# Smaller last pieces of the output projection, alternating stores, and V of three units in two transfers

## The chip, the cores and the metric

The kernel runs on one core of a Trainium2 chip. The metric is the device time of that core in microseconds (us). Each timed execution also has a span, from the first to the last instruction of the program; the time is about 1.8 us longer than the span (187.37 against 185.60 in the profiled run of the kernel before).

Engine names in the profile: PE is TensorE matmul, PEld its weight loads, DVE is VectorE, ACT is ScalarE, POOL is GpSimd, SP is SyncE. A "q" behind an engine's name (SPq, ACTq) marks its sequencer: issues of transfers, waits and branches.

## The reference, cut to what matters

```python
B, Sq, D = 8, 32, 1024;  Hq, Hkv, Sk, Dh = 32, 4, 8192, 128
q = (x @ wq).reshape(B, Sq, Hq, Dh).transpose(0, 2, 1, 3)
k = repeat(k_cache[:, :, Sk - W:, :], rep=8, axis=1)      # W = 2048: a window at the end of the cache
v = repeat(v_cache[:, :, Sk - W:, :], rep=8, axis=1)
p = softmax(einsum("bhqd,bhkd->bhqk", q, k) * Dh ** -0.5)
o = einsum("bhqk,bhkd->bhqd", p, v)
return o.transpose(0, 2, 1, 3).reshape(B, Sq, Hq * Dh) @ wo     # 256 rows x 1024 columns
```

All is bf16. The kernel cuts attention into 32 units, one for each pair of a batch and a KV head.

## The kernel before

For every unit, V (512 KB) is loaded in one transfer and copied by VectorE into an operand with a column of ones beside it:

```python
def load_v(self, ui, eng):
    b, g = self.units[ui]
    self.v_sb[ui] = self.vp.tile([self.P, self.KT, self.Dh], BF16, name="v_sb", tag="v")
    eng.dma_start(out=self.v_sb[ui][:, :, :],
                  in_=self.v_cache[b, g, self.Sk - self.W:, :].rearrange("(p j) d -> p j d", j=self.KT))
```

The output projection adds up over four head groups in an fp32 tile. In the last group a piece of columns is multiplied (8 matmuls into a PSUM tile `ps` from a pool of two), added to what was there, and stored:

```python
            if i == 0:
                st["ps"] = self.open_ps = self.ps_m.tile([P, 512], FP32, name="op_ps", tag="m")   # ps_m: 2 buffers
            # ... two of the piece's eight matmuls ...
            if i == 3 and mm is not True:
                # ...
                    o_t = self.osb.tile([P, 512], BF16, name="o_t")                               # osb: 5 buffers
                    nc.vector.tensor_tensor(out=o_t[:, 0:w], in0=ps[:, 0:w], in1=acc, op=ALU.add)
                    eng = nc.sync if n0 == 0 else nc.scalar
                    eng.dma_start(out=self.out[t * P:(t + 1) * P, n0:n0 + w], in_=o_t[:, 0:w])
```

The last block (the second 128 rows) comes last of all, in three pieces, and a branch stands in it. The kernel computes the softmax without subtracting the maximum; a check over all units decides whether an exact fallback has to run. Every engine passes this branch behind the matmuls of the first piece; with this data the fallback is skipped.

```python
    self.last = self.o_pieces(self.Hkv - 1, 1, (512, 256, 256))
    for p in self.last[:3]:
        p()
    self.last[3](mm=True)            # matmuls of the first piece, ahead of the branch
    # ... branch over the fallback ...
    self.last[3](mm=False)           # its add and store, behind the branch
    for p in self.last[4:]:
        p()
```

## Time and profile before

The first three runs had a median of 187.43 us (187.19 to 187.6). Numbers of the profiled run:

| what | value |
|---|---|
| span | 185.60 us |
| first score matmul starts | 13.65 us |
| start of the first to end of the last score matmul ("the middle") | 160.75 us |
| end of the last score matmul to first matmul behind the branch | 6.08 us |
| first matmul behind the branch to the end ("the tail") | 5.12 us |

The tail of the kernel before in order of time. Columns: start in us, length, engine, line, operation, output and inputs, shapes, count; in brackets the idle time before it and what ended that:

```profile
180.48 1.91 PE L290 MATMUL op_ps<-wo_sb,OT 128*128 128x256 bf16 x16
181.09 0.35 SPq L302 DMA_DIRECT2D out_dram<-o_t  x1
181.55 0.42 DVE L300 TENSOR_TENSOR o_t<-op_ps,oacc 128x256 bf16<-128x256 f32 x1 [0.49 <-PE op_ps L290]
182.01 1.21 ACTq L302 DMA_DIRECT2D out_dram<-o_t  x2
182.42 0.42 DVE L300 TENSOR_TENSOR o_t<-op_ps,oacc 128x256 bf16<-128x256 f32 x1 [0.45 <-PE op_ps L290]
```

The last store is the second of the two ScalarE issues, from 182.88 to 183.22. Its landing, from the list of transfers issued in that window (KB each, then us from issue to landing):

```profile
out_dram<-o_t ACTq DMA_DIRECT2D x1, 64.0 KB, 1.6
```

The trace's records have it to two digits: issued 182.88, landed 184.46. The record of a transfer covers its issue alone (0.34 us). The Trainium skill says so of this kind of transfer ("Perfetto Trace Analysis", section on the HWDGE DMA instruction: the movement of the data is not in the profiled window), and this trace agrees: 1.58 us from issue to landing, more than four times the record. The trace's packet records split these 1.58 us: the first packet starts 0.85 us after the issue began (0.51 us after the record has ended), the packets take 0.34 us, and the landing is seen 0.40 us after the last of them.

```profile
L646 SPq EVENT_SEMAPHORE  x5: 28/28/28, 184.5 to 184.7; - x5
L646 SPq DRAIN  x1: 13/13/13, 184.8 to 184.8; - x1
```

These are five waits: the one that the landing released, and four more whose semaphores were long there.

### The profile page before, as it was taken

To read this page: it belongs to the slowest core of one execution; us is meant where nothing else is said; L and a number is where in the kernel's file an instruction comes from. 1 tells how busy PE (TensorE), PEld (TensorE's weight loads), DVE (VectorE), ACT (ScalarE), POOL (GpSimd) and SP (SyncE) were. 2 spreads that over 40 slices of the span, in tenths; PEclk is the share of its full clock that TensorE was granted. 3 is DMA by queue.
4 is the path that set the end of the run, shared out by engine and by line. 5 is a ranking of instruction groups with operands and counts; after the bars stand their busy time and mean duration, and the time that the engine had idled before them with its cause. 6 is when DMAs were issued, how large, how long until landed. Compare 5 with 4: busy or idle time off the path is not lost. (4 is left out here: it accounts for less than half of the span.)

```text
span 185.6 us, 5054 instructions
## 1 busy us (share of the span) xinstructions
PE 178.8 (96%) x2048; PEld 153.1 (82%) x2064; DVE 115.1 (62%) x267; ACT 131.7 (71%) x133; POOL 94.7 (51%) x150
## 2 busy tenths in 40 slices
PE   7699999999999999999999999999999999999993
PEld 2589999999999999987878999987777888888842
DVE  0128699994586685586467558647746855445372
ACT  2207899787789777777777677787777888888700
POOL 2000007949939959929954980796299189500000
PEclk9999999999999999999999999999999999999999
DMA  6999999999999999999999999999999999930012
GB/s 151 321 397 415 414 415 389 195 270 353 296 274 304 310 320 398 368 240 254 376 323 250 367 349 276 202 409 357 269 371 329 192 326 174 276 96 0 4 62 62
DMA packets 52507, 51.75 MB, mean 279 GB/s; under 512 B 39424, under 2 KB 40064, under 8 KB 52480
## 3 DMA queue, kind: packets, MB, share of 16 engines
q1 hardware_dynamic: 51904, 50.87, 95.6%
q10 hardware_dynamic: 576, 0.52, 0.8%
q8 instruction: 17, 0.28, 0.6%
q14 instruction: 10, 0.08, 0.2%
HBM read 41.42 MB, written 0.52 MB: 226 GB/s over the span
## 5 line engine op out<-in xcount | busy, mean ns | idle before, releaser
L466 ACT ACTIVATE pT<-s_ps 128x1024 bf16<-128x1024 f32 x128 | 128.9, 1025 | 33.3 <-PE s_ps L464 32.3
L256 POOL TENSOR_SCALAR kTv<-kb 32x512 bf16<-32x512 bf16 x140 | 93.7, 670 | 65.4 <-DMA k_raw<-in_k_cache_dram 27.0
L475 PEld LDWEIGHTS <-pT 128*128 128x128 bf16 x1024 | 68.5, 98 | 3.1
L464 PEld LDWEIGHTS <-kT 128*128 128x128 bf16 x368 | 34.8, 98 | 10.3
L290 PE MATMUL op_ps<-wo_sb,OT 128*128 128x512 bf16 (+1 forms) x120 | 32.8, 365 | 0.8
L270 PE MATMUL q_ps<-xT,wq_sb 128*128 128x256 bf16 x192 | 28.2, 273 | 0.0
L475 PE MATMUL o_ps<-va_112,pT 128*128 128x129 bf16 x352 | 27.1, 220 | 0.0
L475 PE MATMUL o_ps<-va_113,pT 128*128 128x129 bf16 x352 | 27.0, 220 | 0.1
L475 PE MATMUL o_ps<-va_114,pT 128*128 128x129 bf16 x320 | 24.7, 220 | 0.0
L246 DVE STREAM_TRANSPOSE kb<-k_raw 128x512 bf16<-128x512 bf16 x36 | 23.8, 684 | 0.0
L412 DVE RECIPROCAL RL_all<-o_ps 128x2 f32<-128x2 f32 x32 | 5.2, 164 | 27.5 <-PE o_ps L475 27.5
L417 DVE TENSOR_SCALAR o_sb<-o_ps,RL_all 128x128 bf16<-128x128 f32 x64 | 19.5, 346 | 1.1
L464 PEld LDWEIGHTS <-kTv 128*128 128x128 bf16 x144 | 13.9, 98 | 5.1
L270 PEld LDWEIGHTS <-wq_sb 128*128 128x128 bf16 x192 | 17.0, 98 | 1.2
L464 PE MATMUL s_ps<-QT_63,kT 128*128 128x256 bf16 x112 | 16.8, 273 | 0.0
L419 DVE STREAM_TRANSPOSE OT<-o_sb 128x256 bf16<-128x256 bf16 x32 | 14.2, 445 | 1.1
L464 PE MATMUL s_ps<-QT_66,kT 128*128 128x256 bf16 x96 | 14.4, 273 | 0.1
L290 PEld LDWEIGHTS <-OT 128*128 128x128 bf16 x136 | 11.1, 98 | 2.8 <-DVEq L77 0.6
L464 PE MATMUL s_ps<-QT_65,kT 128*128 128x256 bf16 x80 | 12.0, 273 | 0.1
L464 PE MATMUL s_ps<-QT_64,kT 128*128 128x256 bf16 x80 | 12.0, 272 | 0.1
L297 DVE TENSOR_TENSOR oacc<-op_ps,oacc 128x512 f32<-128x512 f32 x8 | 5.5, 682 | 7.4 <-PE op_ps L290 7.4
L406 DVE COPY va_113<-v_sb 128x2048 bf16<-128x2048 bf16 x11 | 9.5, 859 | 0.0
(46 smaller groups left out, 104.0 us busy)
## 6 DMA issues: line engine op xcount, KB each, us to landing
v_sb<-in_v_cache_dram SPq DMA_DIRECT2D x32, 512.0 KB, 7.0
wo_sb<-in_wo_dram SPq DMA_DIRECT2D x16, 512.0 KB, 6.3
wq_sb<-in_wq_dram SPq DMA_DIRECT2D x14, 512.0 KB, 7.1
k_raw<-in_k_cache_dram SPq DMA_DIRECT2D x13, 512.0 KB, 5.7
wq_sb<-in_wq_dram SPq DMA_DIRECT2D x4, 256.0 KB, 7.0
kT<-in_k_cache_dram SPq DMA_TRANSPOSE x36, 6.9
k_raw<-in_k_cache_dram SPq DMA_DIRECT2D x2, 256.0 KB, 8.2
x_sb<-in_x_dram ACTq DMA_DIRECT2D x1, 256.0 KB, 3.7
```

The costliest lines, as they stand in the source:

```text
L246: nc.vector.transpose(out=st["kb"][:, sl, :], in_=self.k_raw[ui][:, sl, :])
L256: nc.gpsimd.tensor_scalar(out=out, in0=in_, scalar1=1.0, scalar2=1.0, op0=ALU.mult, op1=ALU.mult)
L270: nc.tensor.matmul(st["ps"][:, 0:self.NQ], lhsT=self.wq_t[g, i][:, c % (DC // 2), hl * P:(hl + 1) * P], rhs=self.xT[:, c, :], start=(c == ...
L290: nc.tensor.matmul(ps[:, 0:w], lhsT=self.OT[:, gq, c, t * P:(t + 1) * P], rhs=self.wo_t[gq][:, c, n0:n0 + w], start=(k == 0), stop=(k == 7))
L297: nc.vector.tensor_tensor(out=acc, in0=ps[:, 0:w], in1=acc, op=ALU.add)
L406: self.nc.vector.tensor_copy(out=self.va[ui % 3][:, :, 0:self.Dh], in_=self.v_sb[ui][:, :, :])
L412: nc.vector.reciprocal(out=rl[:, ui * QT_N:(ui + 1) * QT_N], in_=o_ps[:, :, Dh])
L417: nc.vector.tensor_scalar(out=o_sb[:, qt, :, :], in0=o_ps[:, qt, 0:Dh].rearrange("p (i c) -> p c i", c=4), scalar1=rl[:, ui * QT_N + qt:ui ...
L419: nc.vector.transpose(out=self.OT[:, g * QT_N:(g + 1) * QT_N, :, b * self.Sq:(b + 1) * self.Sq], in_=o_sb[:, :, :, :])
L464: nc.tensor.matmul(s_ps[:, jj, :], lhsT=self.kT[ui][:, c * CJ + jj, :], rhs=q_u, start=True, stop=True)
L466: nc.scalar.activation(out=pT[:, :, :], in_=s_ps[:, :, :], func=ACT.Exp, bias=0.0, scale=self.scale)
L475: nc.tensor.matmul(o_ps[:, qt, 0:self.VW], lhsT=pT[:, jj, qt * P:(qt + 1) * P], rhs=va[:, j, 0:self.VW], start=(j == 0 and qt == 0), stop= ...
```

## The change

Its intent, as far as the code tells: let the last add and the last store be small, so that little stands between the last matmul and the end; spread the stores over two issuing engines; and cut V of the last three units in two. It also rewrites the projection in the fallback as a loop over 32 heads, with another layout for the attention output that it reads; this is a much shorter program that doesn't run here.

```diff
+V_HALVES = 29
     def load_v(self, ui, eng):
-        eng.dma_start(out=self.v_sb[ui][:, :, :],
-                      in_=self.v_cache[b, g, self.Sk - self.W:, :].rearrange("(p j) d -> p j d", j=self.KT))
+        n = self.KT // (2 if ui >= V_HALVES else 1)
+        for j in range(0, self.KT, n):
+            eng.dma_start(out=self.v_sb[ui][:, j:j + n, :],
+                          in_=self.v_cache[b, g, self.Sk - self.W:, :].rearrange("(p j) d -> p j d", j=self.KT)[:, j:j + n, :])
@@ o_pieces
-                    eng = nc.sync if n0 == 0 else nc.scalar
+                    eng = nc.sync if n0 in (0, 768) else nc.scalar
@@ tail_begin
-        self.last = self.o_pieces(self.Hkv - 1, 1, (512, 256, 256))
+        self.last = self.o_pieces(self.Hkv - 1, 1, (512, 256, 128, 128))
@@ out_proj (fallback; cut)
-        with tc.For_i(0, Hkv, 1) as g:
-            # ... 8 heads of a group: one load, one copy, 32 matmuls
+        with tc.For_i(0, Hq, 1) as h:
+            # ... one head: one load, one copy, 4 matmuls
```

More of the change, by code (lines that the diff above doesn't have):

```diff
@@ L580, in attention_exact @@
                 nc.tensor.matmul(o_ps[:, :], lhsT=v_sb[:, j, :], rhs=pT[:, j, :], start=(j == 0), stop=(j == KT - 1))
-            nc.vector.tensor_copy(out=OT_e[:, bass.ds(g * (B * UQ) + b * UQ, UQ)], in_=o_ps[:, :])
+            nc.vector.tensor_copy(out=OT_e[:, :].rearrange("p (g h b s) -> p g h b s", g=Hkv, h=rep, b=B)[:, bass.ds(g, 1), :, bass.ds(b, 1), :],
+                                  in_=o_ps[:, :].rearrange("p (g h b s) -> p g h b s", g=1, h=rep, b=1))
 def out_proj(tc, wo, OT_e, out_flat, fast, *, Hkv, Hq, Sq, NQ, D):
@@ L596, in out_proj @@
         pc = ctx.enter_context(tc.tile_pool(name="pc", bufs=1, space=PSUM))
-        wo_v = wo.rearrange("(g h p) n -> g p h n", p=P, h=rep)
+        wo_v = wo.rearrange("(h p) n -> h p n", p=P)
         acc = accp.tile([P, NT, D], FP32, name="acc")
         nc.vector.memset(acc[:, :, :], 0.0)
-        with tc.For_i(0, Hkv, 1) as g:
-            wo_sb = wop.tile([P, rep, D], BF16, name="wo_sb")
-            nc.sync.dma_start(out=wo_sb[:, :, :], in_=wo_v[bass.ds(g, 1), :, :, :].rearrange("o p h n -> p (o h) n"))
-            o_g = wop.tile([P, rep, B, Sq], BF16, name="o_g")
-            nc.vector.tensor_copy(out=o_g[:, :, :, :].rearrange("p h b s -> p b h s"),
-                                  in_=OT_e[:, bass.ds(g * (B * UQ), B * UQ)].rearrange("p (b h s) -> p b h s", b=B, h=rep))
-            o_v = o_g[:, :, :, :].rearrange("p h b s -> p h (b s)")
-            ps = pc.tile([P, NT, D], FP32, name="ps")
-            for h in range(rep):
-                for t in range(NT):
-                    for n in range(NC_):
-                        nc.tensor.matmul(ps[:, t, n * 512:(n + 1) * 512], lhsT=o_v[:, h, t * P:(t + 1) * P],
-                                         rhs=wo_sb[:, h, n * 512:(n + 1) * 512], start=(h == 0), stop=(h == rep - 1))
+        with tc.For_i(0, Hq, 1) as h:
+            wo_sb = wop.tile([P, D], BF16, name="wo_sb")
+            nc.sync.dma_start(out=wo_sb[:, :], in_=wo_v[bass.ds(h, 1), :, :].rearrange("o p n -> p (o n)"))
+            o_h = wop.tile([P, NQ], BF16, name="o_h")
+            nc.vector.tensor_copy(out=o_h[:, :], in_=OT_e[:, bass.ds(h * NQ, NQ)])
+            ps = pc.tile([P, NT, D], FP32, name="ps")
+            for t in range(NT):
+                for n in range(NC_):
+                    nc.tensor.matmul(ps[:, t, n * 512:(n + 1) * 512], lhsT=o_h[:, t * P:(t + 1) * P],
+                                     rhs=wo_sb[:, n * 512:(n + 1) * 512], start=True, stop=True)
             nc.vector.tensor_tensor(out=acc[:, :, :], in0=ps[:, :, :], in1=acc[:, :, :], op=ALU.add)
```

## The prediction

> What bounds the kernel. The page's busy shares put PE at 178.8 of 185.6 us (96%); in every stretch that I read between 100 and 176 us PE is busy 98 to 100% at a clock of 1.00, and in the view of waits for 100 to 186 us PE waits for nothing. Only the tail is not PE: the last matmul group ends at 182.40, the last add (128x256, 0.42 us) at 182.84, the last store (64 KB, from ScalarE) is issued at 182.9 and lands 1.6 us later, about 184.5; closing waits take the rest to 185.6. So the change can act only by starving PE or on these last 3 us.
>
> V in halves (units 29 to 31). Same bytes, three more issues on SyncE of 0.38 to 0.53 us each (timeline of the DMA issues), rows of 2 KB for 4 KB. The copy into the V operand still waits for both halves, so nothing starts earlier. Issued, landed, copied: V29 148.5, 156.1, 162.2; V30 151.5, 159.9, 164.6; V31 159.7, 163.5, 170.1. The last half of K, issued at 160.3 and landed 164.6, is first read at about 172.5. Slack is 4.7 to 8 us against at most 1.5 us of added issue time: 0 us on the critical path.
>
> Last block 512, 256, 128, 128. 16 matmuls of 128 columns replace 8 of 256. The 256-wide ones are spaced about 0.107 us (16 in 1.91 us, less a 0.17 us pipeline tail), the 129-wide ones of the attention about 0.057 us (8 in 0.62 us): 0.91 us in place of 0.86. But the PSUM pool has two buffers: the fourth piece takes the buffer of the 256 piece, whose add ends at 181.97, while PE would be ready at about 181.80: a new wait of about 0.2 us. Estimate: the fourth piece runs 182.03 to 182.65, its add takes about 0.29 us (0.69 for 512 columns, 0.42 for 256, extrapolated) and ends about 182.95 in place of 182.84. The last add also reuses an output tile (five buffers, now six tiles), whose store, issued at 176.9, has long landed: 0.
>
> Stores. One more of 32 KB on SyncE at about 182.3, the last 32 KB on ScalarE at about 183.0. Before, the ScalarE issues (0.34 us each) stand 0.9 us apart, so alternating removes no queueing. The Trainium skill ("DMA: Bandwidth & Descriptors", Anatomy of one DMA) says the fixed cost of a DMA is mostly completion; the trace agrees: 64 KB lands in 1.6 us, of which the data burst is about 0.6. Half the bytes saves an estimated 0.1 us; its Specifications table says that rows under 512 B are read, modified and written, and the new rows are 256 B, so even that may not come. No run here shows it yet.
>
> The rest of the diff is the fallback branch, not executed on this data; it shortens PE's program by about 56 instructions.
>
> Sum: PE and PSUM wait +0.1, store -0.1 to +0.1, V 0: about +0.05 us. Predicted 187.5 us, range 186.9 to 188.1; faster by over 2%: 1%, within 2%: 98%, slower by over 2%: 1%.
>
> What would show it: V copies within 0.3 us of their times and no new PE wait before 176; last PE group ending near 182.6 after a wait for the 256 add; last add of about 0.29 us ending at 182.8 to 183.0; last landing 1.4 to 1.7 us after issue; span 185.4 to 185.8.
>
> What would make it wrong: the 128 pieces not waiting for PSUM (0.2 us faster); 256-byte rows landing late; the extra SyncE store delaying the closing waits; the shorter program moving an instruction fetch onto the tail.

A sentence in front of "Half the bytes" is cut. It took over for a store from ScalarE what the page "DMA: Bandwidth & Descriptors" of the Trainium skill says of transfers issued by GpSimd, and said that the trace agrees. The trace doesn't: of the 1.58 us of the last store 0.40 us are completion, 0.85 us pass before its first packet, and its packets take 0.34 us, not 0.6. So the estimate of 0.1 us that follows has no source left and is a guess. "Its Specifications table" is the table on that page; it speaks of transfers under 512 B, and I read this as rows.

## More of the kernel before

From the page, the span and the share of PE:

```profile
span 185.6 us, 5054 instructions
...
PE 178.8 (96%) x2048; PEld 153.1 (82%) x2064; DVE 115.1 (62%) x267; ACT 131.7 (71%) x133; POOL 94.7 (51%) x150
```

The same by stretches, kernel before. Columns: stretch in us, its length, then for each engine the busy time and the number of instructions in it, the granted clock, the DMA share and GB/s. I cut the span at the start of the first score matmul, the end of the last one, the first matmul behind the branch, and the end of the last add:

```profile
core 0: us, PE busy (x) PEld busy (x) DVE busy (x) ACT busy (x) POOL busy (x), PEclk, DMA share, GB/s
0.00:13.65 13.65, 11.03 (x103) 7.59 (x104) 2.33 (x7) 2.78 (x5) 0.95 (x10) 1.00 0.87 288
13.65:174.40 160.75, 159.96 (x1891) 140.94 (x1904) 108.29 (x247) 127.90 (x127) 93.74 (x140) 1.00 1.04 294
174.40:180.48 6.08, 5.88 (x45) 3.08 (x43) 3.07 (x11) 1.02 (x1) 0.00 (x0) 1.00 0.13 40
180.48:182.84 2.36, 1.91 (x16) 1.47 (x16) 1.42 (x3) 0.00 (x0) 0.00 (x0) 1.00 0.28 87
182.84:185.60 2.76, 0.00 (x0) 0.00 (x0) 0.01 (x1) 0.00 (x0) 0.00 (x0) 0.94 0.17 51
```

In the middle PE is busy 159.96 of 160.75 us: nothing but PE sets its length. In the last 2.76 us no engine computes.

The chain of waits doesn't show them: its last piece is the last add,

```profile
...
182.42 0.42 DVE o_t L300
```

so the 2.76 us behind that add (2.75 by the records, where the add ends at 182.85) have to be read from the sequencers' own records.

## The result, and the profile after

The changed kernel: 186.65 us median (186.3 to 187.19, 6 runs) against 187.38 us (186.74 to 187.6, 6 runs). Ratio 0.9966, 95% interval 0.9944 to 0.9988. That is clearly under 1, and under the range of 186.9 to 188.1 us that I had given. Ratios here are the mean time of one kernel's runs over the mean of the other's of the same rounds, so they aren't quite the ratio of the medians. Executions over 1.5% slower than the fastest of the same kernel are left out of the means.

The page of the changed kernel:

```profile
span 185.0 us, 5079 instructions
...
PE 179.5 (97%) x2056; PEld 153.7 (83%) x2072; DVE 115.4 (62%) x268; ACT 131.8 (71%) x133; POOL 94.7 (51%) x150
```

PE is busy longer (179.5 against 178.8 us) while the span is shorter. By the same stretches, columns as above:

```profile
0.00:13.32 13.32, 11.60 (x103) 8.02 (x104) 2.33 (x7) 2.88 (x5) 0.95 (x10) 1.00 0.85 283
13.32:174.07 160.75, 159.97 (x1892) 140.95 (x1904) 108.36 (x247) 127.92 (x127) 93.74 (x140) 1.00 1.06 295
174.07:180.15 6.08, 5.88 (x45) 3.07 (x43) 3.07 (x11) 1.02 (x1) 0.00 (x0) 1.00 0.11 36
180.15:182.63 2.48, 2.09 (x24) 1.70 (x24) 1.58 (x4) 0.00 (x0) 0.00 (x0) 1.00 0.29 93
182.63:185.04 2.41, 0.00 (x0) 0.00 (x0) 0.00 (x1) 0.00 (x0) 0.00 (x0) 1.00 0.19 45
```

Set line against line. The middle is the same to the last digit, 160.75 us, and so are the 6.08 us behind it: V in halves did nothing there. The start is 0.33 us shorter. From the first matmul behind the branch to the end of the last add it takes 2.48 us, 0.11 longer by the trace's records (the cut at 182.84 lies 0.01 us ahead of the add's end). From the last add to the end it takes 2.41 us, 0.34 shorter.

The tail in order of time (start, length, engine, line, operation):

```profile
180.15 2.15 PE L293 MATMUL op_ps<-wo_sb,OT 128*128 128x256 bf16 x24
180.75 1.56 SPq L305 DMA_DIRECT2D out_dram<-o_t  x2
181.22 0.74 DVE L303 TENSOR_TENSOR o_t<-op_ps,oacc 128x256 bf16<-128x256 f32 x2 [0.49 <-PE op_ps L293]
181.68 1.33 ACTq L305 DMA_DIRECT2D out_dram<-o_t  x2
181.70 0.43 PEld L293 LDWEIGHTS <-OT 128*128 128x128 bf16 x7 [0.19 <-issue]
182.34 0.29 DVE L303 TENSOR_TENSOR o_t<-op_ps,oacc 128x128 bf16<-128x128 f32 x1 [0.38 <-PE op_ps L293]
```

Instructions of one line that follow each other closely share a row: the VectorE row of 0.74 us is the 256-wide add (0.43 us, to 181.65) and the first 128-wide one behind it; the last add has a row of its own. The 0.19 us before the weight load at 181.70 is the predicted wait of the fourth piece for the PSUM buffer of the second (the view names no releaser; an experiment below confirms it). The fourth piece starts 0.05 us after the 256-wide add has ended. The last store is issued at 182.66 and lands at 184.14:

```profile
out_dram<-o_t ACTq DMA_DIRECT2D x1, 32.0 KB, 1.5
```

And what SyncE does after that landing, between 184.15 and 184.27 us:

```profile
L647 SPq EVENT_SEMAPHORE  x1: 28/28/28, 184.2 to 184.2; - x1
L647 SPq DRAIN  x1: 13/13/13, 184.2 to 184.2; - x1
```

One wait in place of five. Here are the starts of SyncE's eight closing waits as the trace records them (for each the completion semaphore's number; each wait that isn't held up takes 0.06 us from start to start):

```text
semaphore            100     102     104     105     106     107     108     109     then drain   last store on
before            183.37  183.69  183.89  184.48  184.54  184.60  184.66  184.72     184.79      105, landed 184.46
changed kernel    182.36  182.42  182.48  182.54  182.60  183.24  183.46  184.16     184.23      109, landed 184.14
```

The order of the waits is the same in both programs. Before, the last store had the fourth semaphore of the eight, so four waits were still to be passed after its landing. The change adds four transfers (three for V, one store), the turn moves on by four, and the last store has the eighth: no wait is left. Landing to end took 1.14 us before and 0.89 after.

The sum of waits can mislead here: for SyncE the view of waits puts 2.9 us down to the output's landings before and 1.4 us after, but most of those waits run beside the last store and cost nothing. What counts is where the last landing finds SyncE in its list.

### The profile page after: what moved, and what is told of

Same layout as the page of the kernel before. It is cut to its first block, busy times and chain, and to the rows that moved or that the text cites. A ratio compares the mean times of both kernels' runs of the same rounds, so it can differ in the third digit from the quotient of the medians.

```text
span 185.0 us, 5079 instructions
## 1 busy us (share of the span) xinstructions
PE 179.5 (97%) x2056; PEld 153.7 (83%) x2072; DVE 115.4 (62%) x268; ACT 131.8 (71%) x133; POOL 94.7 (51%) x150
## 5 line engine op out<-in xcount | busy, mean ns | idle before, releaser
L293 PE MATMUL op_ps<-wo_sb,OT 128*128 128x512 bf16 (+2 forms) x128 | 33.0, 353 | 0.8
```

The source lines that it names most:

```text
L293: nc.tensor.matmul(ps[:, 0:w], lhsT=self.OT[:, gq, c, t * P:(t + 1) * P], rhs=self.wo_t[gq][:, c, n0:n0 + w], start=(k == 0), stop=(k == 7))
```

## The experiments

All are edits of the kernel before or of the changed kernel, and all gave correct results. The theory, called T in the expectations, is the closing semaphores; its rivals are A (the smaller pieces bring it), B (V in halves arrives earlier), C (the new fallback program) and D (chance at the start).

Every profile was cut at the same five points. All numbers in us:

| run | start | middle | first matmul behind the branch to last add | last add to landing | waits left | landing to end | tail |
|---|---|---|---|---|---|---|---|
| before | 13.65 | 160.75 | 2.37 | 1.61 | 4 | 1.14 | 5.12 |
| before, again | 13.28 | 160.75 | 2.37 | 1.61 | 4 | 1.14 | 5.12 |
| changed | 13.32 | 160.75 | 2.48 | 1.51 | 0 | 0.89 | 4.89 |
| e1 pieces alone | 13.66 | 160.75 | 2.49 | 1.50 | 3 | 1.07 | 5.07 |
| e2 three V halves alone | 13.05 | 160.75 | 2.37 | 1.57 | 1 | 0.95 | 4.89 |
| e3 four V halves alone | 13.92 | 160.75 | 2.37 | 1.57 | 0 | 0.89 | 4.83 |
| e4 five V halves alone | 13.76 | 160.75 | 2.37 | 1.59 | 7 | 1.31 | 5.27 |
| e5 eight V halves alone | 13.80 | 160.75 | 2.37 | 1.62 | 4 | 1.14 | 5.12 |
| e6 changed, halves in the middle | 13.72 | 160.75 | 2.48 | 1.51 | 0 | 0.89 | 4.89 |
| e7 new fallback alone | 12.97 | 160.75 | 2.37 | 1.61 | 4 | 1.14 | 5.11 |
| e8 changed, own PSUM | 13.83 | 160.75 | 2.25 | 1.51 | 0 | 0.90 | 4.66 |
| e9 changed, stores on ScalarE | 13.62 | 160.75 | 2.49 | 1.51 | 0 | 0.90 | 4.90 |

### e1: the pieces and the alternating stores alone

```diff
-                    eng = nc.sync if n0 == 0 else nc.scalar
+                    eng = nc.sync if n0 in (0, 768) else nc.scalar
-        self.last = self.o_pieces(self.Hkv - 1, 1, (512, 256, 256))
+        self.last = self.o_pieces(self.Hkv - 1, 1, (512, 256, 128, 128))
```

> Kernel before with the four pieces and the alternating stores alone; V whole, old fallback. Theory T (closing semaphores): SyncE's closing waits stand in a fixed order, one every 0.06 us, and the last store's completion semaphore is now the fifth of eight (fourth before, eighth in the changed kernel), so three waits are still to be passed after the last landing (four before, none in the changed kernel). From the branch (first matmul after it) to the end: last add +0.12 us, last landing after it -0.10 us, closing waits -0.06 us: together about -0.04 us against before; ratio 0.9995, inside noise. Rival A (smaller last pieces): most of the 0.6 us of the change is here, ratio about 0.997 and a tail 0.3 us shorter. Start of the first score matmul: 13.3 to 13.7 us by chance.

Measured: ratio 0.9994 (0.9974 to 1.0014), tail 5.07 us, three waits left. The named aim of the change is worth 0.05 us: the smaller store saves 0.11, the last add ends 0.12 later for the wait on PSUM, and one closing wait goes. Rival A falls.

### e3: four units of V in halves, nothing else

```diff
+V_HALVES = 28            # load_v as in the change; last block and fallback as before
```

> Kernel before with V of the last four units in halves and nothing else: last block still 512, 256, 256, last store still 64 KB. Its last store gets the eighth of the eight completion semaphores. Theory T: nothing changes until the last landing; after it no wait is left, so the end comes 0.24 us sooner after the last landing than before (0.90 us in place of 1.14 us from landing to end); ratio about 0.9987. Rival A (smaller pieces): no gain. Rival B (V in halves arrives earlier and PE or a copy starts earlier): the gain shows before the last landing, in the time between first score matmul and last matmul (168.7 us before).

Measured: ratio 0.9981 (0.9962 to 1.0001, by time alone not clear of noise), tail 4.83 us. Up to the last add the tail is that of before (2.37 us), the store is still 64 KB, and the end comes 0.24 us sooner after the landing. The other 0.05 us I hadn't expected: the landing itself came sooner, 1.568 us after the last add in place of 1.613, and so it did in e2. That the landing depends a little on which semaphore it posts is possible (1.61 to 1.62 us on the fourth, 1.59 on the first, 1.57 on the seventh and eighth, all with 64 KB), but why isn't shown. The middle is 160.75 us, so nothing of V mattered on the way. The closing line of this run after its last landing, between 184.69 and 184.82 us:

```profile
L649 SPq EVENT_SEMAPHORE  x1: 28/28/28, 184.7 to 184.7; - x1
```

### e4: five units in halves

```diff
+V_HALVES = 27
```

> The same with V of the last five units in halves: the last store gets the first of the eight semaphores. Theory T: seven waits are passed after the last landing, 0.06 us each, so landing to end takes about 1.32 us: 0.18 us longer than before and 0.43 us longer than with four units in halves; ratio about 1.001. Rival B (halves help by arriving earlier): as good as or better than four units, ratio 0.9985 or lower.

Measured: ratio 1.0013 (0.9995 to 1.0031), tail 5.27 us, landing to end 1.31 us. One more transfer of V moves the last store from the last semaphore to the first, and the tail is 0.44 us longer than in e3. No account in which halves of V help by arriving earlier yields this. The closing line of this run after its last landing, between 184.55 and 185.08 us:

```profile
L649 SPq EVENT_SEMAPHORE  x8: 17/28/28, 184.6 to 185.0; - x8
L649 SPq DRAIN  x1: 13/13/13, 185.0 to 185.0; - x1
```

Eight waits stand behind the landing: one released by it, seven left.

### e7: the new fallback alone

```diff
-V_HALVES = 29
+V_HALVES = 99            # and the last block and its stores as before
```

> The changed kernel with the last block and V as before: only the fallback branch differs from the kernel before. Theory T: nothing, ratio 1.000, four waits after the last landing, 1.14 us from landing to end. Rival C (a shorter program moves an instruction fetch): some of the 0.3 us at the start or a shorter gap at the branch shows here, ratio about 0.998. Rival D (chance at the start): the first score matmul falls anywhere between 13.2 and 13.8 us without regard to the kernel.

Measured: ratio 0.9994 (0.9979 to 1.001), tail 5.11 us. The tail is that of before. Its start, 12.97 us, is the earliest of all, and with 13.32 us of the changed kernel it made rival C look possible: both have the new fallback.

### e6: the change, but with V of units 12 to 14 in halves

```diff
-        n = self.KT // (2 if ui >= V_HALVES else 1)
+        n = self.KT // (2 if 12 <= ui < 15 else 1)
```

> The changed kernel, but V of units 12 to 14 in halves in place of units 29 to 31: the same number of transfers, so the last store keeps the eighth completion semaphore, but nothing of V near the end is touched. Theory T (closing semaphores): from the first matmul after the branch to the end as in the changed kernel, 4.9 us (5.12 before), no wait left after the last landing; 160.75 us from first to last score matmul as in all kernels so far. Rival B (late V in halves matters): back to 5.1 us, or the middle longer. Rival C (the new fallback program makes the start shorter; kernels with it started their score matmuls at 12.97 and 13.32 us, kernels with the old one at 13.65 to 13.92): start at 13.4 us or less; rival D (chance): anywhere from 12.9 to 14.

Measured: tail 4.89 us, no wait left, ratio 0.9996 (0.998 to 1.0013). The tail doesn't care where in the program the three extra transfers stand. The start, 13.72 us with the new fallback, speaks against rival C. The ratio was higher than the tail allows for; see the repeats.

### e8: a PSUM bank of its own for the fourth piece

```diff
-                st["ps"] = self.open_ps = self.ps_m.tile([P, 512], FP32, name="op_ps", tag="m")
+                st["ps"] = self.open_ps = (self.ps_m.tile([P, 512], FP32, name="op_ps", tag="m") if n0 < 896 else
+                                           self.ps_t.tile([P, 512], FP32, name="op_ps4"))
     def tail_end(self):
-        self.last[3](mm=False)
-        for p in self.last[4:]:
-            p()
+        with self.tc.tile_pool(name="ps_t", bufs=1, space=PSUM) as self.ps_t:
+            self.last[3](mm=False)
+            for p in self.last[4:]:
+                p()
```

> The changed kernel with the fourth piece in a PSUM bank of its own. If its wait for the 256 add is what made the last add end 0.12 us later, PE runs all 24 matmuls without a gap, the last piece's result is ready 0.23 us sooner and the last add (0.29 us) ends about 2.24 us after the first matmul behind the branch (2.48 in the changed kernel, 2.36 before); from there to the end 4.65 us (4.89 and 5.12); ratio to before about 0.9975. If the wait is not PSUM's (weight loads or the branch), no change. Rival C on the start: 13.4 us or less; rival D: anywhere.

Measured: ratio 0.9969 (0.9955 to 0.9984), tail 4.66 us. The attention's pools are closed by then, so the bank is free. The tail of this run (start, length, engine, line, operation):

```profile
180.66 1.93 PE L294 MATMUL op_ps<-wo_sb,OT 128*128 128x256 bf16 x24
181.26 1.56 SPq L306 DMA_DIRECT2D out_dram<-o_t  x2
181.73 0.74 DVE L304 TENSOR_TENSOR o_t<-op_ps,oacc 128x256 bf16<-128x256 f32 x2 [0.49 <-PE op_ps L294]
182.62 0.29 DVE L304 TENSOR_TENSOR o_t<-op_ps,oacc 128x128 bf16<-128x128 f32 x1 [0.16 <-PE op_ps L294]
```

The 24 matmuls take 1.93 us without a gap (2.15 in the changed kernel) and the last add follows 0.23 us sooner. So the wait was PSUM's. This version has the shortest tail of all. By time it beats the kernel before; against the changed kernel the times don't tell (0.998 and 0.9981 in the one set of rounds that had both, s4 and s1 below).

### e5 and e2: two more counts of halves

```diff
+V_HALVES = 24            # e5: eight units;  e2: 29, three units
```

> Kernel before with V of the last eight units in halves and nothing else: eight more transfers, so the last store gets the same, fourth, completion semaphore as before. Theory T: four waits after the last landing, 5.1 us from the branch to the end, ratio 1.000; the middle stays at 160.75 us. Rival B (halves help in themselves, more halves help more): ratio under 0.9985. Rival C on the start (old fallback): 13.6 us or more; rival D: anywhere.

Measured: ratio 1.0014 (0.9999 to 1.0029), tail 5.12 us. Eight more transfers bring the turn round to the semaphore of before, and the tail is that of before to 0.01 us. This is the control of e3 and e4: more halves, no gain.

> Kernel before with the change's own V halves (three units) alone: the last store gets the seventh semaphore. Theory T: one wait left after the last landing, the end comes 0.18 us sooner after it than before (0.96 in place of 1.14 us). Rival A (smaller last pieces make the gain): none here. Rival C on the start (old fallback): 13.6 us or more; rival D: anywhere.

Measured, a single look: 186.54 us, one wait left, 0.95 us from landing to end; the tail is 4.89 us. The change's V halves alone thus bring all of the change's tail. Its start, 13.05 us with the old fallback, speaks against rival C: starts near 13 us come with both fallbacks. Over all profiles the eight with the old one lie at 13.05 to 13.92 us, the twelve with the new one at 12.97 to 13.83.

### e9: the stores of the last block on ScalarE

```diff
-                    eng = nc.sync if n0 in (0, 768) else nc.scalar
+                    eng = nc.sync if n0 == 0 else nc.scalar
```

> The changed kernel with all stores of the last block but the first on ScalarE, as before the change. Its three issues of 0.34 us would stand at about 1.5, 1.9 and 2.5 us after the first matmul behind the branch; the second would follow the first at once, the last not be held up. So alternating is worth nothing: last landing and end as in the changed kernel, 4.89 us from that matmul to the end. If alternating matters, the last store lands later by up to 0.3 us.

Measured, a single look: 187.22 us with a start of 13.62; tail 4.90 us. Alternating the issuing engine is worth nothing here. The Trainium skill ("DMA: Bandwidth & Descriptors", Issuing engines are not separate DMA queues) says that issuing from several engines saves only the sequencer's time for the issue; the trace agrees, as ScalarE's issues of about 0.34 us never held up the last one.

### The two kernels timed again, and what the rest is

The tail explains 0.23 us of the 0.64 us. In the first profiles the start gave another 0.33: PE waited longer for the first weights of Q. The start of the kernel before (start, length, engine, line, operation, idle before):

```profile
6.82 4.78 PE L372 MATMUL q_ps<-xT,wq_sb 128*128 128x256 bf16 x48 [1.36 <-DMA wq_sb<-in_wq_dram]
...
13.65 0.60 PE L464 MATMUL s_ps<-QT_63,kT 128*128 128x256 bf16 x4
```

and of the changed kernel:

```profile
6.05 1.91 PE L375 MATMUL q_ps<-xT,wq_sb 128*128 128x256 bf16 x16
8.17 2.81 PE L375 MATMUL q_ps<-xT,wq_sb 128*128 128x256 bf16 x32 [0.22 <-DMA wq_sb<-in_wq_dram]
...
13.32 0.60 PE L467 MATMUL s_ps<-QT_63,kT 128*128 128x256 bf16 x4
```

Nothing in the change touches these loads. Whether the start is the program's or chance, the following runs were to tell. All but the last are kernels from above, timed again without any further edit.

> The kernel before, unchanged, timed against itself: how far two sets of five rounds of one program lie apart. Theory (chance at the start): the score matmuls start anywhere from 12.9 to 14.0 us in each execution, so two equal programs show ratios within about 0.9985 to 1.0015 of 1; the tail from the first matmul after the branch to the end is 5.12 us again and the middle 160.75 us.

Measured: the kernel before against itself gives 0.9994 (0.9979 to 1.0008); its start was 13.28 us this time, 13.65 the first time.

> The changed kernel once more. If the 0.64 us of its first measurement were all of the change's making, the ratio is 0.9966 again. Theory: only the tail is of the change's making, 4.89 us in place of 5.12, so the ratio is about 0.9988, plus or minus 0.0015 of chance; the start falls anywhere from 12.9 to 14.0 us.

Measured: the changed kernel, second time: 0.997 (0.9955 to 0.9986), start 12.98. My expectation of 0.9988 was missed by more than I had allowed.

> The changed kernel, third measurement. Chance: ratio about 0.9988 plus or minus 0.0015, and no different from the kernel with the halves in the middle. A property of the program: 0.997 again and clearly below the kernel with the halves in the middle.

Measured: 0.9981 (0.9966 to 0.9996), start 13.75.

> The changed kernel with V of units 12 to 14 in halves, second measurement; tail 4.89 us like the changed kernel's. Chance: ratio about 0.9988 plus or minus 0.0015. A property of the program: 0.9996 again.

Measured: 0.9994 (0.9977 to 1.001), start 13.66, tail 4.89.

> Kernel before with V of the last eight units in halves, second measurement; tail 5.12 us like before. Chance: ratio about 1.000 plus or minus 0.0015. A property of the program: 1.0014 again.

Measured: 1.0008 (0.999 to 1.0026), start 13.40, tail 5.12.

> The changed kernel with a PSUM bank of its own for the fourth piece, second measurement; tail 4.66 us, 0.46 us shorter than before, so a ratio of about 0.9975 plus or minus 0.0015, and about 0.0012 below the changed kernel if the starts come out alike.

Measured: 0.998 (0.9962 to 0.9997), start 13.10, tail 4.66.

> The changed kernel, fourth measurement. Chance: ratio about 0.9988 plus or minus 0.0015. A property of the program: about 0.997, below t2 by 0.002 or more.

Measured: 0.9991 (0.9962 to 1.002), start 13.33, tail 4.89. This is nearer to the number named for chance than to that of a property of the program, but its interval holds both.

> The changed kernel with V of units 12 to 14 in halves, third measurement, same tail. Chance: about 0.9988 plus or minus 0.0015, like t1. A property of the program: about 0.9995.

Measured: 0.9995 (0.9968 to 1.0022), start 13.41, tail 4.89.

The last run gets the eighth semaphore without any halves of V, by cutting three loads of output weights:

```diff
-V_HALVES = 29
+V_HALVES = 99
-            self.nc.sync.dma_start(out=self.wo_t[gq][:, 2 * i:2 * i + 2, :],
-                                   in_=self.wo[...].rearrange("(p c) n -> p c n", c=4)[:, 2 * i:2 * i + 2, :])
+            n = 1 if gq == 7 or (gq, i) == (6, 1) else 2
+            for c in range(2 * i, 2 * i + 2, n):
+                self.nc.sync.dma_start(out=self.wo_t[gq][:, c:c + n, :],
+                                       in_=self.wo[...].rearrange("(p c) n -> p c n", c=4)[:, c:c + n, :])
```

> The changed kernel with V whole; three loads of output weights (the last tile's two and one of the tile before) are cut in two instead, so that the last store has the eighth completion semaphore again. Closing theory: tail 4.89 us, no wait after the last landing, middle 160.75 us. If late V halves are worth 0.3 us by themselves, the ratio is about 0.9995 like the kernel with the halves in the middle; if halves in the middle cost 0.3 us, or all is chance, it is at or under 0.9988.

Measured: 0.9991 (0.9967 to 1.0016), tail 4.89 us, no wait left, start 13.27. For the tail, three cut weight loads serve as well as three halves of V; the ratio lies between the two numbers that I had named and decides nothing.

What follows. Here are the measurements grouped by their tail, beside what the tail alone predicts, namely 1 plus the difference to 5.12 us over 187.2 us:

| tail, us | kernels | ratios measured | mean | from the tail alone |
|---|---|---|---|---|
| 5.27 | e4 | 1.0013 | 1.0013 | 1.0008 |
| 5.11 to 5.12 | before again, e5 twice, e7 | 0.9994, 1.0014, 1.0008, 0.9994 | 1.0003 | 1.0000 |
| 5.07 | e1 | 0.9994 | 0.9994 | 0.9997 |
| 4.89 | changed four times, e6 three times, weight loads cut | 0.9966, 0.997, 0.9981, 0.9991; 0.9996, 0.9994, 0.9995; 0.9991 | 0.9986 | 0.9988 |
| 4.83 | e3 | 0.9981 | 0.9981 | 0.9985 |
| 4.66 | e8 twice | 0.9969, 0.998 | 0.9975 | 0.9975 |

The means follow the tail. Within the row of 4.89 us the changed kernel's own mean is 0.9977, that of e6 0.9995. Their profiles agree in every stretch but the start (12.98 to 13.75 us in four profiles against 13.41 to 13.72 in three), and on the two chips on which both were timed together their intervals overlap widely (0.9966 to 0.9996 against 0.9977 to 1.001; 0.9962 to 1.002 against 0.9968 to 1.0022). So about 0.2 us of the changed kernel's mean gain over four measurements isn't explained by its tail. Less the tail's 0.23 us the four measurements leave 0.41, 0.33, 0.13 and -0.06 us, in the order in which they were taken. That it belongs to the program isn't shown, that it is chance isn't either. It stays open.

## Why the prediction was wrong, point by point

- "0 us on the critical path" for V in halves: right for what I meant by it. The middle was 160.75 us in every profile, and the V copies of the last three units came at 161.90, 164.29 and 169.72 us, each 0.33 us earlier than before, exactly as much as the start. But three more transfers also move the turn of the completion semaphores, and that was worth three closing waits at the very end.
- The last block: right. A wait for PSUM "of about 0.2 us" was 0.19 in the trace's view, the last add took 0.29 us, and it ended 0.11 us later than before, counted from the first matmul behind the branch; I had 0.11 too. e8 shows that the cause is the one named.
- Stores: "-0.1 to +0.1"; the trace has -0.10 (1.61 us from the last add to the landing before, 1.51 after), at the edge of what I had said. That is partly luck: the sentence cut above had the make-up of a store wrong. With half the bytes the packets took 0.26 us in place of 0.34, and the completion behind them 0.37 in place of 0.40; the 0.85 us before the first packet stayed. The parts don't add up cleanly either: the pieces alone brought -0.11 (e1), the halves of V alone -0.05 (e2, with the store unchanged), both together -0.10. Alternating was worth nothing, as said.
- The step that failed is "closing waits take the rest to 185.6". I carried the time behind the landing, 1.14 us, over as a constant. It is made of 0.89 us that is constant (0.89 to 0.90 in all profiles without a wait left) and of 0.06 us for each closing wait that stands behind the last store's semaphore: four before, none after, -0.24 us (1.136 to 0.894). Of the ways to be wrong I had named "the extra SyncE store delaying the closing waits"; what happened is the opposite sign.
- The sum then: +0.11 - 0.10 - 0.24 = -0.23 us, in place of "+0.05". The trace's tails, 4.89 against 5.12 us, say the same.
- The range was too narrow for the rest. A tail of -0.23 us alone would have left 187.2 us, inside it. The measured 186.65 us lies 0.55 us lower; by the ratio, which compares runs of the same rounds, 0.41 us of the 0.64 are not the tail's. In the profiled pair the start alone differs by 0.33 us; my sum had no term for the start, and whether the change moves it stays open. Over all 20 profiles the first score matmul fell between 12.97 and 13.92 us, one and the same program ranging from 12.98 to 13.75. The three runs that I based the range on spread over 0.41 us and had a median of 187.43; the kernel before, measured along with the later runs, had medians of 187.02 to 187.38 us.

## What to carry to other kernels

When PE is busy to the last and the gain is sought in the tail, read the closing instructions of every sequencer too: they lie on the critical path, the chain of waits doesn't show them, and adding a transfer anywhere can change them, because it decides which completion semaphore the last store gets. Counting the program's transfers tells which one before anything runs: the expectations of e1 to e5 named it, and all five were right. So in this kernel the last store belongs on the semaphore that is waited for last. And when a last piece is cut smaller, count the buffers: with two PSUM buffers the fourth piece gave back here what the smaller store had gained, and a bank of its own took another 0.23 us off the tail.

## What the Trainium skill lacked or had wrong

- "Runtime: NRT & Kernel Launch", The ~15µs preamble/postamble breakdown: it lists barriers and semaphore resets behind a kernel, but not the program's own waits for its transfers' completion semaphores. Here there are eight in a fixed order, 0.06 us apart, and landing to end takes 0.89 us with none left and 1.31 us with seven left.
- "DMA: Bandwidth & Descriptors", Specifications: transfers under 512 B are said to be read, modified and written, which my prediction read as rows. In these runs the store with rows of 256 B (32 KB) landed 1.48 us after its issue and that with rows of 512 B (64 KB) 1.58 us. In the packet records of these two stores a row of 256 B took 17.6 ns on average and one of 512 B 26.8 ns: two thirds of the time for half the bytes. So the small rows moved their bytes more slowly, but a small row didn't take longer than a large one; whether a read came with it these records don't tell.
- The same page, Anatomy of one DMA: its fixed cost of about 2.0 us, most of it completion, is given for transfers issued by GpSimd; my prediction carried the remark about completion over to ScalarE, where it didn't hold. For the last stores issued by ScalarE the whole time from issue to landing was 1.47 to 1.58 us here: 0.84 to 0.85 us up to the first packet, 0.26 to 0.35 us of packets, and 0.34 to 0.40 us from the last packet to the landing.
- None of the pages that I read says that a program's transfers take completion semaphores in turn and that the place in that turn can show in the time: tails of 4.83 to 5.27 us, from nothing but four or five V loads cut in two.
